# Attention and two feed-forward layers on one core: low part of x by PE and ACT for the first 8 units, word loads in turn, and layer 1's blocks 0 and 1 in two passes of steps

## The chip, the cores and the metric

The kernel runs on one core of a Trainium2 chip. The metric is the device time of one launch in microseconds (us). The engines are TensorE (PE, with its weight loads as PEld), VectorE (DVE), ScalarE (ACT), GpSimd (POOL) and SyncE (SP). SP and ACT issue the transfers (DMA) of this kernel; their queues are shown as SPq and ACTq. Each engine works through its own instructions in order.

## The reference

A linear attention with a decaying state, then two feed-forward layers, all in fp32:

```python
# q, k, v, alpha: (batch 4, heads 8, seq 768, head_dim 48)
state = alpha[:, :, t, :, None] * state + einsum('bhd,bhe->bhde', k[:, :, t], v[:, :, t])
y[:, :, t] = einsum('bhd,bhde->bhe', q[:, :, t], state)

x = y.transpose(0, 2, 1, 3).reshape(3072, 384)
h = x @ moe_w_in          # (384, 2048)
x = maximum(0.01 * h, h) @ moe_w_out
h = x @ moe2_w_in
out = where(h > 0, h, exp(minimum(h, 0)) - 1) @ moe2_w_out
```

## The kernel before, in words

**Units.** The attention is done in 24 units of 128 positions of one batch row (6 units a row, all 8 heads at once). A unit's inputs are a `pack` (alpha, k and q) and a `vt` (v); three buffers of each go round. Per unit, DVE scans alpha backward (`E`) and forward (`F`) and scales k and q with the scans; PE forms the scores (`sc`, two banks), turns k round (`pk`), and DVE masks the scores into `A`. PE multiplies A with v, and q with the carried state `T`, into `po`; k and v into `pu`, the state's increment. ACT copies `pk` (to `kn`) and casts `po` to the high part of x (`attn_xh`); DVE subtracts that from `po` to the low part (`attn_xl`). PE's fp32 products are made of such high and low parts (three products: high by high, low by high, high by low). All small PSUM results of a unit share three banks in turn (`ps_a`), so `pu` of the next unit takes the bank that `po` gives up.

**Quarters.** The first 8 units are written out by hand in `quarter(u, i)`, four quarters a unit; each prepares the next unit while it finishes its own. Units 0 to 3 (block 0) run ahead of all else, together with the conversions of the first weights. When a block's four units are done, `gather` moves 6 slices of x from partition to partition by DMA, since the heads do not fill the partitions.

**Steps.** A block is 512 rows of x. Layer 1 takes each block through 16 steps `m` of 128 of the 2048 inner columns: `ffn1_h` (nine products into `hp`), `ffn1_t` (ACT, 0.01 h), `ffn1_max` (DVE), `ffn1_gh` (ACT, high part), `ffn1_gl` (DVE, low part), and `ffn1_y` (nine products that add to three banks `y` over all 16 steps). At the last step `y` is copied to `x2t[block]`. The list `seq` holds the order of steps; PE does `ffn1_y` of step s and `ffn1_h` of step s + 2. There are 6 blocks, then layer 2 with 16 steps each likewise.

**Words.** The weights come as raw fp64 words and are converted on the chip, one step's w_in and w_out at a time: `stage1(m)` loads the words of step m with five DMAs on SP's queue, `convert_p` makes two passes on ACT, `convert_a` three instructions on DVE and ACT's cast to the high part, `convert_b` one subtraction on DVE for the low part. Layer 1's words are loaded into the tiles `x2t[0]` to `x2t[3]`, four steps in flight; `x2t[4]` and `x2t[5]` are scratch. The first sixteen steps, all of block 0, convert the words of the step that comes four later, and the quarters of block 1 are strewn among them (13 quarters over 14 steps). From the second block on all weights are there, and the units of the next block are strewn among the steps of a block.

Up to the end of that hand-made part, `in_order()` ties each engine to the order in which the code is written; behind it a scheduler may move instructions.

Of the kernel before, what the change touches and what calls it, by code (L numbers as in the profile page):

```python
# [10 lines left out]
I32 = mybir.dt.int32  # L11
# [8 lines left out]
def attention_two_layers_kernel(  # L20
# [42 lines left out]
    causal = const.tile([128, C], F32, name="causal")  # L63
    d0 = const.tile([PR, EXT], F32, name="d0")
# [19 lines left out]
    def constants():  # L84
        make_identity(nc, ident)
        nc.gpsimd.memset(causal, 1.0)
        nc.gpsimd.affine_select(
            out=causal, in_=causal, compare_op=ALU.is_ge, fill=0.0,
            base=0, pattern=[[1, C]], channel_multiplier=-1,
        )  # L90
        nc.vector.memset(d0, 0.0)
        nc.vector.memset(d0[:, 0:EXT:C + 1], 1.0)
        nc.vector.memset(d1, 0.0)
        nc.vector.memset(bias[:, 0:1], -1.0)
        nc.vector.memset(bias[:, 1:2], -ALPHA_SPAN)
        nc.vector.memset(far_sum[:, 1:2], 1.0)
# [144 lines left out]

    def attn_state(u):
        c = u % NC
        d = st[u]
        if c < NC - 1:
            Sn = at_p.tile([PR, NP, D], F32, tag="S", name="S")
            if c > 0:
                nc.vector.tensor_add(Sn, d["pu"], d["T"])
            else:
                nc.vector.tensor_copy(Sn, d["pu"])  # L250
            st["S"] = Sn
# [74 lines left out]

    def ffn1_y(j, m):
        n = xt[j][2]
        gh, gl = steps.pop((1, j, m))
        if m == 0:  # L330
            ytiles[j] = [ps_y.tile([128, n], F32, tag=f"y{c}", name=f"y{c}") for c in range(KD)]
        wh, wl = wout[m]
        for c in range(KD):
            for i, (a, x) in enumerate(((wh, gh), (wl, gh), (wh, gl))):
                nc.tensor.matmul(  # L335
                    ytiles[j][c], lhsT=a[:, c * 128:(c + 1) * 128], rhs=x,
                    start=(m == 0 and i == 0), stop=(m == KF - 1 and i == 2),
                )
        if m == KF - 1:
            t0 = blocks[j][0] * C  # L340
            dst = x2t[t0 // 512][:, :, t0 % 512:t0 % 512 + n]
            for c in range(KD):
                if c == 1:
                    nc.vector.tensor_copy(dst[:, c], ytiles[j][c])
                else:
                    nc.scalar.copy(dst[:, c], ytiles[j][c])
# [113 lines left out]
    def stage1(m, eng=None):  # L460
        t = x2t[m % 4].rearrange("p c f -> p (c f)").bitcast(I32)
# [42 lines left out]
    class Conversions:  # L504
# [20 lines left out]
        def b(self, upto):  # L525
            for i in range(self.done[2], min(upto, self.done[1])):
# [3 lines left out]
                if self.layer == 1 and m + 4 < KF:  # L530
                    stage1(m + 4)
# [121 lines left out]
    with ExitStack():  # L653
# [8 lines left out]
        for m in range(1, 4):  # L662
            stage1(m)
# [7 lines left out]
        def quarter(u, i, chain=True):  # L671
# [13 lines left out]
            elif i == 2:  # L685
# [6 lines left out]
                next_load(u + 3)  # L692
            else:
                attn_xl(u, xh, xl, off)
# [8 lines left out]
        for u in range(UB):  # L703
            for i in range(3):
                quarter(u, i)
            if u > 1:
                conv1.a(u - 1)
# [9 lines left out]
        quarter(UB, 1)  # L717
        conv1.b(UB - 1)
        ffn1_max(0, 0)
        ffn1_gh(0, 0)  # L720
        quarter(UB, 2)
        ffn1_h(0, 1)
        ffn1_t(0, 1)
        ffn1_gl(0, 0)
        conv1.p(UB)
        ffn1_max(0, 1)
        ffn1_gh(0, 1)
# [3 lines left out]
        seq = [(1, j, m) for j in range(NB) for m in range(KF)]  # L731
# [10 lines left out]
        for s, e in enumerate(seq):  # L742
# [3 lines left out]
            if s < KF:  # L746
# [9 lines left out]
                conv1.b(s + 4)  # L756
                ffn1_gl(n[1], n[2])
                conv1.p(s + 5)
                in_order()
                continue  # L760
            if ph == 1 and pieces:
                tgt = blocks[j + 1][1] * 4
                done = tgt - len([p for p in pieces if unit_block[p[0]] <= j + 1])
                want = min(tgt, -(-tgt * (m + 1) // (KF - LA)))
# [123 lines left out]
```

## Time and profile before

| | |
|---|---|
| time, median of 3 runs | 975.14 us (974.55 to 976.91) |
| the profiled execution | 976.15 us, span 974.4 us |
| PE busy | 922.9 us (95%) |
| PEld busy | 779.2 us (80%) |
| DVE busy | 532.4 us (55%) |
| ACT busy | 445.9 us (46%) |
| mean granted clock of PE | 0.974 |
| read from HBM, written | 54.37 MB, 4.72 MB |

The span runs from the first to the last instruction of the profiled execution; its own time is 1.75 us more. Busy shares are means over stages that have different limits. The granted clock is a share of 2.4 GHz; it has two levels, 1.2 and 2.4 GHz, so that 0.79 over a stretch is a mixture of both.

### The profile page before, as it was taken

How to read it: one execution, taken by the hardware profiler on the slowest of the kernel's cores; microseconds unless marked ns; L12 is line 12 of the kernel's file. 1: busy time of each engine (PE TensorE's matmuls, PEld its weight loads, DVE VectorE, ACT ScalarE, POOL GpSimd, SP SyncE). 2: the span in 40 equal slices, each digit the busy share in tenths (PEclk: the TensorE clock that was granted, in tenths of full speed). 3: DMA queues.
4: the chain of work that ended last, by engine and by line, in shares of the span. 5: the costliest groups of instructions: out<-in, count | busy, mean ns of one | idle time of the engine just before them, and what ended most of it. 6: DMA issues, size and time to landing. Idle time of an engine off the chain costs nothing.

```text
span 974.4 us, 13128 instructions
## 1 busy us (share of the span) xinstructions
PE 922.9 (95%) x5234; PEld 779.2 (80%) x5234; DVE 532.4 (55%) x876; ACT 445.9 (46%) x783; POOL 1.1 (0%) x8
## 2 busy tenths in 40 slices
PE   5678889999999999999999999999999999999996
PEld 4555666888788788788888889999999999899995
DVE  6769894855746556545369993433433433433332
ACT  1235653322322222233367795474564654644442
POOL 0000000000000000000000000000000000000000
PEclk9688998999999999999999999999999999999998
DMA  9664523113111212211134430020110200100001
GB/s 247 161 160 135 165 74 89 42 41 90 49 41 42 57 41 83 57 41 49 33 114 133 127 90 18 1 81 1 47 34 1 71 10 1 62 1 0 33 1 37
DMA packets 25093, 62.38 MB, mean 64 GB/s; under 512 B 3936, under 2 KB 7008, under 8 KB 25024
## 3 DMA queue, kind: packets, MB, share of 16 engines
q1 hardware_dynamic: 19184, 40.54, 14.8%
q10 hardware_dynamic: 5840, 20.92, 7.7%
q8 instruction: 43, 0.70, 0.3%
q14 instruction: 26, 0.21, 0.1%
HBM read 54.37 MB, written 4.72 MB: 61 GB/s over the span
## 4 chain that ended last, share of the span: by engine, by line
PE 84%; DVE 6%; DMA 6%; issue 1%; SPq 1%; ACT 1%; DVEq 0%; ACTq 0%
PE hp L364 21%; PE y L335 18%; PE hp L297 18%; PE oa L395 10%; PE o L395 10%; DMA x2t<-in_w_dram 2%; PE sc L158 2%; PE po L212 2%; PE po L218 2%; DMA vt<-in_vals_dram 2%; DVE x2t L276 1%; DVE x2t L278 1%; DMA pack<-in_seqs_dram 1%; DMA x<-x 1%; DVE x2t L275 1%
## 5 line engine op out<-in xcount | busy, mean ns | idle before, releaser
L297 PE MATMUL hp<-x,w 128*128 128x512 f32 x864 | 219.6, 397 | 14.8 <-DMA x<-x 7.4
L364 PE MATMUL hp<-x,w 128*128 128x512 f32 x864 | 215.4, 393 | 0.0
L297 PEld LDWEIGHTS hp<-x,w 128*128 128x128 f32 x864 | 162.2, 190 | 54.3 <-DVE w L282 8.0
L364 PEld LDWEIGHTS hp<-x,w 128*128 128x128 f32 x864 | 160.7, 188 | 29.3
L335 PE MATMUL y<-gh,w 128*128 128x512 f32 x576 | 179.8, 400 | 0.0
L373 DVE SCALAR_TENSOR_TENSOR t<-t,hp 128x512 f32<-128x512 f32 x96 | 65.9, 686 | 148.1 <-ACT t L372 148.1
L335 PEld LDWEIGHTS y<-gh,w 128*128 128x128 f32 x576 | 106.9, 191 | 23.5 <-issue 1.1
L303 ACT ACTIVATE t<-hp 128x512 f32<-128x512 f32 x96 | 57.2, 596 | 125.8 <-PE hp L297 125.6
L312 ACT CAST gh<-t 128x512 fp32r<-128x512 f32 x96 | 59.6, 621 | 113.3 <-PE y L335 61.7
L335 PE MATMUL y<-gl,w 128*128 128x512 f32 x288 | 109.9, 395 | 0.0
L308 DVE TENSOR_TENSOR t<-t,hp 128x512 f32<-128x512 f32 x96 | 65.4, 681 | 78.6 <-ACT t L303 78.6
L81 DVE TENSOR_TENSOR gl<-t,gh 128x512 fp32r<-128x512 f32 x96 | 66.4, 692 | 70.6 <-ACT gh L78 68.9
L371 ACT ACTIVATE t<-hp 128x512 f32<-128x512 f32 x96 | 57.1, 595 | 104.7 <-PE hp L364 104.7
L395 PE MATMUL oa<-w,gh 128*128 128x384 f32 x384 | 96.7, 337 | 0.0
L395 PE MATMUL o<-w,gh 128*128 128x384 f32 x384 | 94.6, 336 | 0.0
L318 DVE TENSOR_TENSOR gl<-t,gh 128x512 fp32r<-128x512 f32 x96 | 66.1, 689 | 47.6 <-ACT gh L312 44.6
L78 ACT CAST gh<-t 128x512 fp32r<-128x512 f32 x96 | 59.5, 620 | 64.7 <-PE oa L395 34.8
L395 PEld LDWEIGHTS o<-w,gh 128*128 128x128 f32 x384 | 70.6, 188 | 5.4
L395 PEld LDWEIGHTS oa<-w,gh 128*128 128x128 f32 x384 | 70.2, 188 | 2.9
L335 PEld LDWEIGHTS y<-gl,w 128*128 128x128 f32 x288 | 54.5, 189 | 12.1
L395 PE MATMUL oa<-w,gl 128*128 128x384 f32 x192 | 63.0, 337 | 0.0
L372 ACT ACTIVATE t<-t 128x512 f32<-128x512 f32 x96 | 60.8, 633 | 2.3
(91 smaller groups left out, 833.0 us busy)
## 6 DMA issues: line engine op xcount, KB each, us to landing
pack<-in_seqs_dram ACTq DMA_DIRECT2D x21, 674.2 KB, 5.6
stg<-in_w_dram SPq DMA_DIRECT2D x28, 384.0 KB, 3.2
x2t<-in_w_dram SPq DMA_DIRECT2D x20, 384.0 KB, 3.8
vt<-in_vals_dram ACTq DMA_DIRECT2D x21, 288.0 KB, 5.6
span<-in_seqs_dram SPq DMA_DIRECT2D x24, 226.2 KB, 2.6
x2t<-in_w_dram SPq DMA_DIRECT2D x32, 144.0 KB, 2.8
out_dram<-osb SPq DMA_DIRECT2D x24, 192.0 KB, 2.1
x<-x SPq DMA_DIRECT2D x36, 64.0 KB, 4.4
```

The costliest lines, as they stand in the source:

```text
L78: nc.scalar.copy(dst, src)
L81: (lo_engine or nc.vector).tensor_sub(lo, src, dst.bitcast(F32))
L297: nc.tensor.matmul(hp, lhsT=a[:, kk, :], rhs=x[:, kk, :n], start=(i == 0), stop=(i == 3 * KD - 1))
L303: nc.scalar.activation(t, steps[1, j, m], ACTF.Copy, scale=0.01)
L308: nc.vector.tensor_max(t, t, hp)
L312: nc.scalar.copy(gh, steps[1, j, m][0])
L318: nc.vector.tensor_sub(gl, t, gh.bitcast(F32))
L335: nc.tensor.matmul(ytiles[j][c], lhsT=a[:, c * 128:(c + 1) * 128], rhs=x, start=(m == 0 and i == 0), stop=(m == KF - 1 and i == 2),)
L364: nc.tensor.matmul(hp, lhsT=a[:, kk, :], rhs=x[:, kk, :], start=(i == 0), stop=(i == 3 * KD - 1))
L372: nc.scalar.activation(t, t, ACTF.Exp, scale=-1.0)
L373: nc.vector.scalar_tensor_tensor(out=t, in0=t, scalar=-1.0, in1=hp, op0=ALU.add, op1=ALU.max)
L395: nc.tensor.matmul(otiles[j][i], lhsT=a[:, i * 128:(i + 1) * 128], rhs=x, start=(m == 0 and n == 0), stop=(m == KF - 1 and n == 2),)
```

## The change

For units 0 to 7 the low part of x is no longer a DVE subtraction: PE adds the product of `minus` (the identity times -1) and the high part to `po` (`attn_rest`), and ACT copies what is left (`attn_xl_act`). The loads of the following units go to SP's queue. Only the words of step 0 are asked for ahead of the units; those of steps 1 to 3 follow one unit at a time, and from step 4 on two tiles, `x2t[2]` and `x2t[3]`, take turns. `hp` of step 1 stands ahead of the rest of unit 4.

The steps of layer 1 run as block 0 steps 0 to 3, block 1 steps 0 to 3, block 0 steps 4 to 15, block 1 steps 4 to 15. Blocks 0 and 1 therefore leave `y` twice: behind step 3 it is copied to `x2t[block]` by ACT, behind step 15 DVE adds it to that. All 13 quarters of block 1 stand in the first two entries of `seq`, and the 12 words left are converted in the entries 2 to 16, three in four. Block 2's units begin one entry later.

```diff
+        nc.scalar.activation(minus, ident[0:PR, 0:PR], ACTF.Copy, scale=-1.0)
...
+    def attn_rest(u, xh, off):
+        nc.tensor.matmul(st[u]["po"], lhsT=minus, rhs=xh[0:PR, :, off:off + C], start=False, stop=True,
+                         skip_group_check=True)
+
+    def attn_xl_act(u, xl, off):
+        nc.scalar.copy(xl[0:PR, :, off:off + C], st[u]["po"])
...
+    FIRST = 4
+
+    def parts(j, m):
+        return m == 0 or (j < 2 and m == FIRST), m == KF - 1 or (j < 2 and m == FIRST - 1)
...
-                if c == 1:
+                if j < 2 and m == KF - 1:
+                    nc.vector.tensor_add(dst[:, c], ytiles[j][c], dst[:, c])
+                elif c == 1 and j > 1:
                     nc.vector.tensor_copy(dst[:, c], ytiles[j][c])
                 else:
                     nc.scalar.copy(dst[:, c], ytiles[j][c])
...
-        t = x2t[m % 4].rearrange("p c f -> p (c f)").bitcast(I32)
+        t = x2t[m if m < 4 else 2 + m % 2].rearrange("p c f -> p (c f)").bitcast(I32)
...
-                if self.layer == 1 and m + 4 < KF:
-                    stage1(m + 4)
+                if self.layer == 1 and m >= 2 and m + 2 < KF:
+                    stage1(m + 2)
...
                 attn_xh(u, xh, off)
-                next_load(u + 3)
+                attn_rest(u, xh, off)
+                load_unit(u + 3)
+                load_v(u + 3)
             else:
-                attn_xl(u, xh, xl, off)
+                attn_xl_act(u, xl, off)
...
-        seq = [(1, j, m) for j in range(NB) for m in range(KF)]
+        head, tail = range(FIRST), range(FIRST, KF)
+        seq = [(1, j, m) for ms in (head, tail) for j in range(2) for m in ms]
+        seq += [(1, j, m) for j in range(2, NB) for m in range(KF)]
...
-            if s < KF:
+            if s <= KF:
+                c = 4 if s == 0 else 1 + FIRST + s - 2 - (s - 2) // 4 if s > 1 and s % 4 != 1 else 0
                 ffn1_y(j, m)
                 pe_h(n)
                 ffn1_t(n[1], n[2])
-                conv1.a(s + 4)
-                if s < KF - LA:
-                    for p in quarters[13 * s // (KF - LA):13 * (s + 1) // (KF - LA)]:
+                conv1.a(c)
+                if s < 2:
+                    for p in quarters[7 * s:7 * s + 7]:
```

Three places in the order of instructions show what moves. The first is DVE in the steps of layer 1, just behind the last quarters of unit 4. Names: `x2t` are words and scratch of a conversion, `w` the weights' parts, `t`, `gh` and `gl` those of a step, `x` the low part of a unit. Before, two conversions with a unit's scan behind the second:

```order
L275 TENSOR_SCALAR x2t_138<-x2t_134 128x768
L276 SCALAR_TENSOR_TENSOR x2t_138<-x2t_138 128x768
L278 ISA x2t_138<-x2t_134,x2t_138 128x1536
L240 TENSOR_TENSOR x<-po,x 112x4x128
L308 TENSOR_TENSOR t<-t,hp 128x512
L282 TENSOR_TENSOR w_4_111<-x2t_138,w_4_110 128x768
L318 TENSOR_TENSOR gl<-t,gh 128x512
L275 TENSOR_SCALAR x2t_139<-x2t_135 128x768
L276 SCALAR_TENSOR_TENSOR x2t_139<-x2t_139 128x768
L278 ISA x2t_139<-x2t_135,x2t_139 128x1536
L127 SCALAR_TENSOR_TENSOR E<-pack,d_96 112x517
```

With the change, the conversion of step 6 and what follows it:

```order
L284 TENSOR_SCALAR x2t_139<-x2t_137 128x768
L285 SCALAR_TENSOR_TENSOR x2t_139<-x2t_139 128x768
L287 ISA x2t_139<-x2t_137,x2t_139 128x1536
L317 TENSOR_TENSOR t<-t,hp 128x512
L291 TENSOR_TENSOR w_6_116<-x2t_139,w_6_115 128x768
L327 TENSOR_TENSOR gl<-t,gh 128x512
L317 TENSOR_TENSOR t<-t,hp 128x512
L327 TENSOR_TENSOR gl<-t,gh 128x512
L284 TENSOR_SCALAR x2t_140<-x2t_138 128x768
```

The subtraction for x and the scans of a unit are gone from between the conversions, and a step without a conversion (`t`, `gl` alone) has come in.

The second place is DVE in unit 2, the first unit with a conversion (`pack` is q being scaled, `E` the scan of unit 4). Before:

```order
L144 TENSOR_TENSOR pack<-pack,F 112x512
L275 TENSOR_SCALAR x2t_138<-x2t_134 128x768
L276 SCALAR_TENSOR_TENSOR x2t_138<-x2t_138 128x768
L278 ISA x2t_138<-x2t_134,x2t_138 128x1536
L240 TENSOR_TENSOR x<-po,x 112x4x128
L282 TENSOR_TENSOR w_0_103<-x2t_138,w_0_102 128x768
L127 SCALAR_TENSOR_TENSOR E<-pack,d_96 112x517
```

Now:

```order
L146 TENSOR_TENSOR pack<-pack,F 112x512
L284 TENSOR_SCALAR x2t_139<-x2t_135 128x768
L285 SCALAR_TENSOR_TENSOR x2t_139<-x2t_139 128x768
L287 ISA x2t_139<-x2t_135,x2t_139 128x1536
L291 TENSOR_TENSOR w_0_104<-x2t_139,w_0_103 128x768
L129 SCALAR_TENSOR_TENSOR E<-pack,d_97 112x517
```

Only the subtraction for x is gone; the conversion's last instruction now stands right behind its third.

The third place is SP's queue around the gather of block 1 (`x<-x`). Before, the words of the last step stand ahead of it and words of layer 2 behind:

```order
L467 DMA x2t_136<-in_w_dram 128x768
L465 DMA x2t_137<-in_w_dram 48x768
L466 DMA x2t_137<-in_w_dram 16x768
L465 DMA x2t_137<-in_w_dram 48x768
L466 DMA x2t_137<-in_w_dram 16x768
L467 DMA x2t_137<-in_w_dram 128x768
L262 DMA x<-x 16x2x512 x6
L481 DMA x2t_139<-in_w_dram 128x768 x2
```

Now the loads of units 9 and 10 stand ahead of it, and words of step 6 behind:

```order
L113 DMA pack<-in_seqs_dram 112x1541
L118 DMA vt<-in_vals_dram 128x576
L113 DMA pack<-in_seqs_dram 112x1541
L118 DMA vt<-in_vals_dram 128x576
L271 DMA x<-x 16x2x512 x6
L482 DMA x2t_137<-in_w_dram 48x768
L483 DMA x2t_137<-in_w_dram 16x768
```

The gather has moved ahead of ten steps' words, and directly behind two units' loads.

## Rows read from the trace of the kernel before

**Rows 1.** Busy time by stretch: length, busy us and count per engine, granted clock, DMA, GB/s

```profile
0.00:66.49 66.49, 38.89 (x358) 30.82 (x359) 46.54 (x79) 15.48 (x22) 1.14 (x8) 0.79 0.81 207
66.49:167.71 101.22, 85.86 (x433) 65.10 (x432) 81.65 (x117) 53.17 (x77) 0.00 (x0) 0.92 0.39 112
167.71:966.00 798.29, 798.11 (x4446) 683.26 (x4444) 403.68 (x681) 377.04 (x684) 0.00 (x0) 1.00 0.16 46
```

**Rows 2.** Waits of PE, 0 to 210 us: us in total, times, longest

```profile
PE pk L166 <- DVE A L180: 10.6, 3, 4.6
...
PE hp L297 <- DVE w L282: 5.8, 4, 2.1
```

**Rows 3.** Timeline, steps of block 0: start, duration, instruction, idle before and releaser

```profile
102.30 0.55 DVE L275 TENSOR_SCALAR x2t<-x2t 128x768 int32<-128x768 int32 x1
...
102.49 2.20 PE L297 MATMUL hp<-x,w 128*128 128x512 f32 x9
...
106.57 2.20 PE L297 MATMUL hp<-x,w 128*128 128x512 f32 x9
...
107.60 0.55 DVE L275 TENSOR_SCALAR x2t<-x2t 128x768 int32<-128x768 int32 x1
```

**Rows 4.** Timeline, units 0 to 3

```profile
16.29 1.16 PE L158 MATMUL sc<-pack 48*128 48x128 f32 x16
16.41 0.58 ACT L237 CAST x<-po 112x512 fp32r<-112x512 f32 x1 [1.31 <-PE po L212]
...
17.64 1.23 DVE L127 TENSOR_TENSOR_SCAN E<-pack,d 112x517 f32<-112x517 f32 x1
...
20.05 1.28 DVE L180 TENSOR_TENSOR A<-sc,causal 128x512 f32<-128x512 f32 x2
...
30.08 1.23 DVE L127 TENSOR_TENSOR_SCAN E<-pack,d 112x517 f32<-112x517 f32 x1 [3.15 <-DMA pack<-in_seqs_dram]
...
32.49 1.28 DVE L180 TENSOR_TENSOR A<-sc,causal 128x512 f32<-128x512 f32 x2
...
42.58 1.28 DVE L180 TENSOR_TENSOR A<-sc,causal 128x512 f32<-128x512 f32 x2
```

**Rows 5.** Timeline, gathers of blocks 0 and 1 and the hp behind each

```profile
47.63 0.32 ACTq L111 DMA_DIRECT2D pack<-in_seqs_dram  x1
...
49.11 3.93 SPq L262 DMA_DIRECT2D x<-x  x6
...
54.95 4.77 PE L297 MATMUL hp<-x,w 128*128 128x512 f32 x9 [5.15 <-DMA x<-x]
...
156.59 3.78 SPq L262 DMA_DIRECT2D x<-x  x6
...
159.68 0.47 PE L297 MATMUL hp<-x,w 128*128 128x512 f32 x1 [0.68 <-DMA x<-x]
```

**Rows 6.** Timeline of DVE, unit 3: low part and end of a conversion

```profile
48.40 0.68 DVE L240 TENSOR_TENSOR x<-po,x 112x512 fp32r<-112x512 f32 x1
49.38 0.96 DVE L282 TENSOR_TENSOR w<-x2t,w 128x768 fp32r<-128x768 f32 x1 [0.30 <-ACT w L279]
```

**Rows 7.** The stretch of unit 1, and T's product there and in unit 4

```profile
17.64:30.08 12.44, 8.47 (x84) 6.96 (x84) 6.30 (x13) 2.80 (x4) 0.00 (x0) 0.58 1.02 256
...
23.62 1.95 PE L218 MATMUL po<-pack,T 48*48 48x128 f32 x16
...
61.11 1.08 PE L218 MATMUL po<-pack,T 48*48 48x128 f32 x16
```

**Rows 8.** Issues of one word; landing of words, 66 to 150 and 12 to 30 us

```profile
72.61 0.31 SPq L465 DMA_DIRECT2D x2t<-in_w_dram  x1
...
74.36 0.42 SPq L467 DMA_DIRECT2D x2t<-in_w_dram  x1
...
x2t<-in_w_dram SPq DMA_DIRECT2D x9, 384.0 KB, 3.6
...
x2t<-in_w_dram SPq DMA_DIRECT2D x3, 384.0 KB, 6.1
```

More of the change, by code (lines that the diff above doesn't have):

```diff
@@ L63, in attention_two_layers_kernel @@
     causal = const.tile([128, C], F32, name="causal")
+    minus = const.tile([PR, PR], F32R, name="minus")
     d0 = const.tile([PR, EXT], F32, name="d0")
@@ L329, in ffn1_y @@
         gh, gl = steps.pop((1, j, m))
-        if m == 0:
+        first, last = parts(j, m)
+        if first:
             ytiles[j] = [ps_y.tile([128, n], F32, tag=f"y{c}", name=f"y{c}") for c in range(KD)]
@@ L336, in ffn1_y @@
                     ytiles[j][c], lhsT=a[:, c * 128:(c + 1) * 128], rhs=x,
-                    start=(m == 0 and i == 0), stop=(m == KF - 1 and i == 2),
+                    start=(first and i == 0), stop=(last and i == 2),
                 )
-        if m == KF - 1:
+        if last:
             t0 = blocks[j][0] * C
@@ L661, in attention_two_layers_kernel @@
         load_v(2)
-        for m in range(1, 4):
-            stage1(m)
         order1 = [("both", m) for m in range(KF)]
@@ L705, in attention_two_layers_kernel @@
                 quarter(u, i)
+            if u < 3:
+                stage1(u + 1)
             if u > 1:
@@ L717, in attention_two_layers_kernel @@
         quarter(UB, 1)
+        ffn1_h(0, 1)
+        ffn1_t(0, 1)
         conv1.b(UB - 1)
+        quarter(UB, 2)
         ffn1_max(0, 0)
         ffn1_gh(0, 0)
-        quarter(UB, 2)
-        ffn1_h(0, 1)
-        ffn1_t(0, 1)
+        ffn1_max(0, 1)
+        ffn1_gh(0, 1)
         ffn1_gl(0, 0)
         conv1.p(UB)
-        ffn1_max(0, 1)
-        ffn1_gh(0, 1)
         ffn1_gl(0, 1)
         in_order()
-        seq = [(1, j, m) for j in range(NB) for m in range(KF)]
+        head, tail = range(FIRST), range(FIRST, KF)
+        seq = [(1, j, m) for ms in (head, tail) for j in range(2) for m in ms]
+        seq += [(1, j, m) for j in range(2, NB) for m in range(KF)]
         seq += [(2, j, m) for j in range(NT // 512) for m in range(KF)]
@@ L755, in attention_two_layers_kernel @@
                 ffn1_gh(n[1], n[2])
-                conv1.b(s + 4)
+                conv1.b(c)
                 ffn1_gl(n[1], n[2])
-                conv1.p(s + 5)
+                if c:
+                    conv1.p(c + 1)
                 in_order()
@@ L761, in attention_two_layers_kernel @@
             if ph == 1 and pieces:
-                tgt = blocks[j + 1][1] * 4
-                done = tgt - len([p for p in pieces if unit_block[p[0]] <= j + 1])
-                want = min(tgt, -(-tgt * (m + 1) // (KF - LA)))
+                nb = max(j + 1, 2)
+                tgt = blocks[nb][1] * 4
+                done = tgt - len([p for p in pieces if unit_block[p[0]] <= nb])
+                i, of = (s - KF, KF - LA - 1) if s < 2 * KF else (m + 1, KF - LA)
+                want = min(tgt, -(-tgt * i // of))
                 now, pieces = pieces[:max(0, want - done)], pieces[max(0, want - done):]
```

## The prediction

> **What bounds the kernel now.** I read the busy times by stretch first. From 167.71 to 966 us TensorE (PE) is busy in 798.1 of 798.3 us at the full granted clock [rows 1]: nothing that leaves that work unchanged can gain or lose there. What can move lies ahead of it. Up to 66.49 us, where the first product with w_out starts, PE is busy 38.89 us at a granted clock of 0.79; from there to 167.71 us, the end of block 0's sixteen steps, 85.86 of 101.22 us at 0.92, while VectorE (DVE) is busy 81.65 us [rows 1].
>
> The waits of PE say on whom it waits: most on DVE's mask A (10.6 us ahead of pk alone) and on DVE's low part of the weights (5.8 us) [rows 2]. So DVE sets the pace of the first 167 us. A step of layer 1, y and hp, costs PE 4.08 us, from one hp to the next (102.49 to 106.57) where nothing else lies between; DVE goes from one conversion to the next in 5.30 us (102.30 to 107.60), with no attention in between but one low part of x [rows 3]. Sixteen such steps plus the attention of block 1 make the 101 us.
>
> **The early units.** I take the order of the change and put the durations of the trace on it.
> Unit 0: the low part on DVE needs po and ACT's copy of it (at 16.41), and only behind it E of unit 2 runs, at 17.64; A of unit 1 follows at 20.05 [rows 4]. With the low part gone from DVE, E to T are done while PE is still at po, and A(1) can start when sc(1) is there, which runs from 16.29 for 1.16 us [rows 4]: A(1) at 17.5, 2.55 us gained.
> Unit 1: E of unit 3 waits 3.15 us for its pack, until 30.08 [rows 4]. ACT issued its load behind the words of four steps; now it stands on SP's queue ahead of all words but the first, and its buffer has been free since unit 0's products. That wait goes. But PE now has to do the product with minus (of 512 columns, 0.47 us for one such alone [rows 5]), and ACT the copy (0.58 us, as the x cast [rows 4]), before pu may take po's bank; before, one subtraction on DVE (0.68 us [rows 6]) did it. I charge 1.0 us per unit where PE's chain sets the pace, as it now does in unit 1. Chain: A(1) 17.5, pu 19.3, pk 20.3, po and the product with T 3.9 us, sc 2.0 us, A(2) at 26.3 instead of 32.49: 6.2 us gained.
> Units 2 and 3: nothing. From A(2) to A(3) are 10.09 us, all DVE with one conversion [rows 4]. There the low part runs from 48.40, behind the third instruction of a conversion, and the conversion's last starts at 49.38 after 0.30 us more of waiting for ACT's cast [rows 6]. The low part is inside a wait that stays; taking it away frees no time.
> The first products come in another order, gl(0,0) now behind the maximum of step 1; by durations that costs 0.5 us. So y(0,0) starts at 66.49 - 6.2 + 0.5 = 60.8 us.
>
> **Steps 0 and 1** now hold 13 quarters of block 1's attention, which were spread over 14 steps. Little else is there to do meanwhile, so it is a chain. From y(0,0): DVE has gl 0.6, conversion 2.65, E to T 2.4, A(5) 0.7 to its first half: 6.9 us with gaps. Then pk, po, T's product and sc: 4.4 us at the full clock, 7.0 us at half (T's product: 1.08 against 1.95 us [rows 7]). Then product with minus, copy and pu 1.75 to 2.15; pk and po 2.15 to 3.0; y(0,1) and hp(0,3) 4.1 to 8; sc 1.16 to 2.1; and behind hp(0,3) ACT's t, x, PE's product, ACT's copy, pu, po, T's product, x and the last product with minus 5.7 to 7. Sum: 26.2 us at the full clock, 36 at half. In the units before, up to 66.49 us, the granted clock is 0.79 [rows 1], that is 42% of the time at 1.2 GHz and the rest at 2.4; 26.2 + 0.42 x 9.8 = 30.3. The steps' products make this one denser, so I take 29.3: y(0,2) at 90.1 us.
>
> **The gather.** hp of (block 1, step 0) is now the product right behind y(0,2). It needs block 1's x, whose last low part ends 0.7 us after y(0,2) begins. Block 0's gather, issued at 49.11 with a pack in flight since 47.63, let hp start at 54.95, 5.84 us later, and that hp took 4.77 us; block 1's, issued at 156.59 with no such load near, let the first go at 159.68, 3.09 us later [rows 5]. In the new order the loads of units 9 and 10 stand right ahead of the gather on SP's queue, and the last of them can only be issued when unit 7 has used its pack, some 2 us before. So I take 5.84: hp(1,0) ends at 90.1 + 0.7 + 5.84 + 4.77 = 101.4 us; without a wait it would be 94.2. The Trainium skill, "DMA: Bandwidth & Descriptors", section "Queues, rings and completion order", says that a copy's semaphore increment lands only after every earlier write of that DMA engine, on any of its queues. By that rule the gather waits out the loads ahead of it; the two gathers of the trace agree (5.84 against 3.09 us). With 3.09 the sum would be 2.75 us better.
>
> **Steps 2 to 16** convert 12 words in 15 steps, three steps in four, with no attention. DVE needs 5.1 to 5.3 us from conversion to conversion [rows 3] (the low part of x lay in the wait for ACT's cast there too), and 1.9 us in the step without one (two instructions of 0.6 us and the wait for gh): 3 x 5.2 + 1.9 = 17.5 us against PE's 16.3, so 4.38 a step. From the end of hp(1,0) to the end of y in step 15 there are 12.5 steps: 54.8 us; if DVE is hidden, 51. ACT has six copies of y more (0.58 us each, as its copy of po [rows 4]), in steps 3 and 7 ahead of its other work; PE waits for y's banks there, 1.7 us as I lay it out. Sum 56.5: step 15 ends at 157.9 us.
> Words: two buffers now instead of four. A word's fifth and last piece is issued 1.75 us behind its first and lands 3.6 us later [rows 8]; with 1.8 us of ACT's two passes and 1.1 us of DVE until the buffer is free again, that is 8.3 us a buffer, 4.15 a word, and 5.2 are to be had. At nothing, therefore; the cover is 1 us a word. The three DVE additions per block in place of copies, 0.7 us each, fall in steps without conversion: nothing.
>
> **Sum.** 167.7 - 157.9 = 9.8 us, less 0.3 for the one conversion left in step 16: 9.5. The attention of block 2 starts a step later, under a full PE, at nothing (if it were late, PE would wait on A, as in [rows 2]). The profiled execution took 976.15 us (span 974.4); with the change 966.65, which against the median of 975.14 is 965.6 us.
>
> **Rivals.**
> All goes well (957 to 961 us): the gather lands in 3.1 us and DVE hides under PE at 4.08 a step: 2.75 + 3.8 us better, 959.1. For it: PE runs ahead by two steps, so a slow step is evened out; against it: the DVE sum is above PE's. Chance 0.2.
> The clock stays low (972.3 us): all of steps 0 and 1 at 1.2 GHz, 36 instead of 29.3 us. For it: 0.58 in the stretch of unit 1, where PE also works in bursts [rows 7]; against it the 0.79 of all units. The Trainium skill, "TensorE: Matmul & The Clock Gate", Part 1, calls the low clock the default that only activity releases; the trace agrees in the 0.58 and, since 0.79 is not 0.5, not in all of it. Chance 0.1.
> The words come late, slower than before: if a landing takes 6.3 us rather than 3.6, a buffer turns in 11 us, a word in 5.5 us, and 12 words take 66 us instead of 56.5, which eats all 9.5; that is the point from which it decides. At 7.2 us, twice the 3.6, a word takes 5.95 us, 12 words 71.4, and the time is 965.6 + 14.9 = 980.5 us. For it: 6.1 us for the same pieces in that crowded stretch; against it: 3.6 between 66 and 150 us, where words are asked for as fast [rows 8]. Chance 0.07.
> The order gains nothing, since the attention was hidden below the steps and is now bare: steps 0 and 1 cost 29.3 us where they cost 9.5, and the rest must win that back at 4.38 a step. It is dead if the steps with conversions still take 5.3 us and more each: 12.5 x 5.3 = 66 us, 975 us, no change. Chance 0.08.
> My forecast with its own range, 962 to 970, holds 0.55.
>
> **Numbers.** 965.6 us; 957 to 971.5 leaves out about 2 in 10. A difference within 0.3% (2.9 us) can hardly be told from none. Faster 0.85, same 0.08, slower 0.07.
>
> **What would show it.** A(2) near 26 us and E(3) without a wait for pack; y(0,0) near 61; y(0,2) near 90 with A and sc alternating in PE's waits; one wait of PE for x of 5 to 8 us near 92 to 100; conversions 5.1 to 5.3 us apart with a longer pause in each fourth step; no wait of ACT for words behind 100 us; step 15's y done near 158, and from there the same row of products as before. Wrong if ACT waits for words, if DVE's steps are longer than 5.3, or if the attention chain of steps 0 and 1 is far from 29 us.

## The result, and the profile after

| | before | after |
|---|---|---|
| median | 974.86 us (974.55 to 976.91, 4 runs) | 961.69 us (960.84 to 961.84, 4 runs) |
| profiled execution, span | 976.15, 974.4 us | 960.84, 959.1 us |
| last product ends at | 965.83 us | 952.30 us |

The ratio of the times is 0.9859, 95% interval 0.9842 to 0.9876: 13.2 us faster by the medians. The two profiled executions differ by 15.3 us; their last products by 13.5. The other 1.8 lie behind the last product (8.57 us before, 6.80 after), where only the output is copied out and lands, so I compare at the last product.

The busy time by stretch of the kernel after, cut where its steps cut it: the start of y of step 0 of block 0, which I write y(0,0), the start of y(0,2), the end of hp(1,0), and the end of y of the sixteenth entry of the list of steps. Columns: length, then busy us and count of PE, PEld, DVE, ACT, POOL, the granted clock, DMA, GB/s.

```profile
0.00:61.25 61.25, 42.14 (x363) 32.20 (x363) 44.02 (x76) 18.30 (x29) 1.14 (x8) 0.80 0.76 197
61.25:85.52 24.27, 20.33 (x192) 15.35 (x192) 22.66 (x37) 10.50 (x17) 0.00 (x0) 1.00 0.50 124
85.52:95.74 10.22, 6.79 (x20) 4.77 (x19) 3.08 (x4) 1.10 (x2) 0.00 (x0) 0.76 0.76 211
95.74:151.33 55.59, 53.73 (x225) 42.12 (x224) 45.71 (x61) 38.91 (x59) 0.00 (x0) 0.98 0.39 114
151.33:959.10 807.77, 798.94 (x4446) 683.14 (x4445) 414.55 (x696) 381.05 (x689) 0.00 (x0) 1.00 0.16 48
```

Beside [rows 1], y(0,0) comes 5.24 us earlier (61.25 against 66.49), and the sixteen entries that follow take 90.08 us instead of 101.22: 16.38 us. From there to the last product it takes 800.97 us where it took 798.12, so 2.85 are given back, and 13.53 remain. In the second stretch DVE is busy 22.66 of 24.27 us: the attention of three units has become a chain that leaves DVE almost no gap, at a full clock.

The timeline of DVE in units 1 to 3, which answers to [rows 4, 6] (start, duration, instruction, idle before and releaser):

```profile
18.84 1.29 DVE L182 TENSOR_TENSOR A<-sc,causal 128x512 f32<-128x512 f32 x2 [1.05 <-PE sc L160]
...
23.45 1.23 DVE L129 TENSOR_TENSOR_SCAN E<-pack,d 112x517 f32<-112x517 f32 x1 [1.33 <-DMA pack<-in_seqs_dram]
...
25.86 1.28 DVE L182 TENSOR_TENSOR A<-sc,causal 128x512 f32<-128x512 f32 x2
...
32.66 0.96 DVE L291 TENSOR_TENSOR w<-x2t,w 128x768 fp32r<-128x768 f32 x1 [0.90 <-ACT w L288]
...
35.95 1.28 DVE L182 TENSOR_TENSOR A<-sc,causal 128x512 f32<-128x512 f32 x2
```

A of unit 1 now waits for its scores, so PE's chain paces there; A of unit 2 starts at 25.86. From A(2) to A(3) it is 10.09 us, to the hundredth what it was: the low part did lie in a wait, and that wait is now the 0.90 us ahead of L291.

The gather of block 1 and hp(1,0) behind it, with the loads ahead of them ([rows 5] had block 0's gather behind a pack, and a gather with nothing near):

```profile
84.55 0.31 SPq L113 DMA_DIRECT2D pack<-in_seqs_dram  x1
84.91 0.43 SPq L118 DMA_DIRECT2D vt<-in_vals_dram  x1
86.33 3.79 SPq L271 DMA_DIRECT2D x<-x  x6
...
91.17 4.57 PE L306 MATMUL hp<-x,w 128*128 128x512 f32 x9 [3.43 <-DMA x<-x]
```

DVE in the steps with conversions, the last of three and the step without one ([rows 3] had 5.30 us from conversion to conversion):

```profile
103.70 0.55 DVE L284 TENSOR_SCALAR x2t<-x2t 128x768 int32<-128x768 int32 x1
...
109.92 0.69 DVE L317 TENSOR_TENSOR t<-t,hp 128x512 f32<-128x512 f32 x1 [1.05 <-ACT t L312]
111.30 0.69 DVE L327 TENSOR_TENSOR gl<-t,gh 128x512 fp32r<-128x512 f32 x1 [0.69 <-ACT gh L321]
111.91 0.56 DVE L284 TENSOR_SCALAR x2t<-x2t 128x768 int32<-128x768 int32 x1
...
116.83 0.56 DVE L284 TENSOR_SCALAR x2t<-x2t 128x768 int32<-128x768 int32 x1
...
121.93 0.56 DVE L284 TENSOR_SCALAR x2t<-x2t 128x768 int32<-128x768 int32 x1
```

Conversions stand 5.10 us apart (116.83 to 121.93), and 8.21 across the step without one (103.70 to 111.91), in which DVE waits 1.05 and 0.69 us for ACT. Four entries thus take DVE 18.23 us (103.70 to 121.93), 4.56 each. PE doesn't wait for that from the start: it stands idle for only 1.86 of the 55.59 us of this stage, and the y of its second entry and of the fifth, three entries on, stand 12.24 us apart, 4.08 an entry, which is PE's own pace in [rows 3]:

```profile
100.64 0.61 PE L350 MATMUL y<-gh,w 128*128 128x512 f32 x2
...
112.88 0.61 PE L350 MATMUL y<-gh,w 128*128 128x512 f32 x2
```

The waits of PE from 0 to 200 us, beside [rows 2], and the two places behind the sixteenth entry where time is given back:

```profile
PE sc L160 <- DVE pack L146: 8.7, 1, 8.7
PE hp L306 <- DMA x<-x: 6.6, 4, 3.4
...
PE pk L168 <- DVE A L182: 2.4, 1, 2.4
```

```profile
151.79 2.64 PE L306 MATMUL hp<-x,w 128*128 128x512 f32 x9 [0.46 <-ACT w L288]
...
156.89 2.65 PE L306 MATMUL hp<-x,w 128*128 128x512 f32 x9 [0.41 <-ACT w L288]
...
181.10 0.70 PE L350 MATMUL y<-gh,w 128*128 128x512 f32 x2 [1.11 <-DVE x2t L359]
```

The wait for A ahead of pk fell from 10.6 to 2.4 us; what PE waits for most, after the first scores, is now the gather.

### The profile page after: what moved, and what is told of

Same layout as the page of the kernel before. It is cut to its first block, busy times and chain, and to the rows that moved or that the text cites. A ratio compares the mean times of both kernels' runs of the same rounds, so it can differ in the third digit from the quotient of the medians.

```text
span 959.1 us, 13157 instructions
## 1 busy us (share of the span) xinstructions
PE 921.9 (96%) x5242; PEld 777.6 (81%) x5242; DVE 530.0 (55%) x872; ACT 449.9 (47%) x794; POOL 1.1 (0%) x8
## 4 chain that ended last, share of the span: by engine, by line
PE 83%; DVE 6%; DMA 4%; ACT 4%; issue 1%; SPq 1%; DVEq 0%; ACTq 0%
PE hp L381 21%; PE y L350 17%; PE hp L306 17%; PE oa L412 11%; PE o L412 11%; DMA pack<-in_seqs_dram 3%; PE po L214 2%; PE sc L160 2%; PE po L220 2%; DVE x2t L285 1%; DVE x2t L287 1%; DVE E L129 1%; PE pu L233 1%; ACT w L288 1%; ACT x2t L279 1%
## 5 line engine op out<-in xcount | busy, mean ns | idle before, releaser
L381 PEld LDWEIGHTS hp<-x,w 128*128 128x128 f32 x864 | 160.7, 188 | 29.3
L82 DVE TENSOR_TENSOR gl<-t,gh 128x512 fp32r<-128x512 f32 x96 | 66.5, 692 | 70.0 <-ACT gh L79 68.4
```

The lines of the kernel that those rows point to most:

```text
L82: (lo_engine or nc.vector).tensor_sub(lo, src, dst.bitcast(F32))
L381: nc.tensor.matmul(hp, lhsT=a[:, kk, :], rhs=x[:, kk, :], start=(i == 0), stop=(i == 3 * KD - 1))
```

## The experiments

All kernels are the changed kernel with one edit, unless a line says more, and all compute the whole result. Each ratio is to the kernel before on the same chip, with its 95% interval. The stages are those of the first table of the profile after, from each kernel's profiled execution; entry 15 is the sixteenth of the list. In the two rows marked one pass the sixteen entries are all of block 0, and one figure stands for them together.

| kernel | median us | ratio (interval) | y(0,0) at | steps 0 and 1, clock | to end of hp(1,0) | to end of entry 15 |
|---|---|---|---|---|---|---|
| changed | 961.69 | 0.9859 (0.9842, 0.9876) | 61.25 | 24.27, 1.00 | 10.22 | 55.59 |
| f1, changed again | 961.84 | 0.9869 (0.9846, 0.9893) | 57.62 | 25.07, 0.93 | 9.99 | 55.56 |
| e1, low part on DVE | 974.26 | 0.9978 (0.9964, 0.9992) | 62.47 | 32.24, 0.82 | 11.31 | 55.56 |
| e2, loads as before | 971.10 | 0.9944 (0.9922, 0.9966) | 67.52 | 27.86, 0.82 | 10.30 | 55.58 |
| e3, one pass | 972.71 | 0.9962 (0.9946, 0.9978) | 57.71 | 108.47 together | | |
| h4, one pass and low part on DVE | 969.96 | 0.9938 (0.9920, 0.9956) | 62.94 | 100.35 together | | |
| e4, gather first | 958.42 | 0.9820 (0.9797, 0.9843) | 56.47 | 27.86, 0.82 | 10.13 | 55.59 |
| f3, gather by two queues | 959.57 | 0.9860 (0.9832, 0.9889) | 56.51 | 25.10, 0.93 | 11.64 | 55.57 |
| f2, ACT's passes late | 958.66 | 0.9832 (0.9813, 0.9851) | 58.83 | 27.85, 0.82 | 11.00 | 54.06 |
| f4, low part of w on GpSimd | 968.65 | 0.9941 (0.9918, 0.9963) | 57.10 | 25.10, 0.93 | 11.15 | 60.85 |
| h1, e4 and f3 | 955.25 | 0.9784 (0.9766, 0.9803) | 56.94 | 24.26, 1.00 | 10.02 | 55.84 |
| h2, h1 and f2 | 952.39 | 0.9758 (0.9738, 0.9778) | 56.49 | 25.12, 0.93 | 9.31 | 53.97 |
| h3, h2 and y(0,3) first | 951.14 | 0.9744 (0.9725, 0.9762) | 56.27 | 24.27, 1.00 | 10.39 | 51.75 |

In h3 hp(1,0) and hp(1,1) run as one group, so the last two columns are cut one hp later; together they are 62.14 us, against 63.28 in h2.

**The same kernel again (f1).** No edit.

> The changed kernel itself, unedited, beside the others of this group on the same chip and with more runs, since its first runs were made elsewhere. Expected 961.7 us, the ratio to before 0.986; where its steps 0 and 1 meet the low clock, as in the run with the gather first, they take 27 to 28 us instead of 24.3.

The time repeats, the early part doesn't: y(0,0) lies at 57.62 in this execution and at 61.25 in the other. Here E of unit 3 starts at 21.30 us with no wait, there at 23.45 with 1.33 us for its pack. So differences of up to 3.6 us in y(0,0) between single profiles say nothing about an edit. From the end of hp(1,0) to the end of entry 15 the executions agree to 0.03 us.

**The low part back on DVE (e1).**

```diff
                 attn_xh(u, xh, off)
-                attn_rest(u, xh, off)
...
-                attn_xl_act(u, xl, off)
+                attn_xl(u, xh, xl, off)
```

> The changed kernel with the low part of x of units 0 to 7 back on VectorE (no product with minus, no copy by ACT); all else as changed. My theory: the move pays only where DVE is not converting (units 0 and 1, 2.5 us, less about 1 us for the longer chain of PE and ACT) and a little in steps 0 and 1: 963 to 964 us, A of unit 2 near 27.5 us instead of 25.9. Rival, that the low part is the main gain of the early units: 966 us or more. Rival, that the product and the copy cost what they save: 961.7, as changed.

A miss by 10 us: nearly the whole gain is gone. In the early units it costs about what the prediction had it for, 6.2 us less the 3.15 of the pack: A(2) comes at 28.80 us, 2.9 us behind the first execution of the changed kernel and 5.1 behind f1; y(0,0) comes at 62.47, 1.2 and 4.9 us behind. But the larger loss stands in steps 0 and 1, 32.24 us against 24.27 and 25.07, where I had looked for little. DVE there, e1 (x<-po is the low part, L129 the next unit's scan E, which is queued behind it):

```profile
74.39 0.69 DVE L242 TENSOR_TENSOR x<-po,x 112x512 fp32r<-112x512 f32 x1 [1.94 <-ACT x L239]
...
86.61 0.69 DVE L242 TENSOR_TENSOR x<-po,x 112x512 fp32r<-112x512 f32 x1 [4.14 <-ACT x L239]
87.22 1.23 DVE L129 TENSOR_TENSOR_SCAN E<-pack,d 112x517 f32<-112x517 f32 x1
...
95.45 0.69 DVE L242 TENSOR_TENSOR x<-po,x 112x512 fp32r<-112x512 f32 x1 [2.55 <-ACT x L239]
```

DVE stands still for ACT's copy of po, and the scans of the next unit stand behind it. In the changed kernel DVE goes from one unit to the next with no wait longer than 0.4 us (0.74 in f1). The clock of e1 is low there too, 0.82. Three kernels with 0.82 in these steps and the low part off DVE (e2, e4, f2) take 27.86 us; an estimate from these is that of the 8 us 4.4 are the order on DVE (32.24 - 27.86) and 3.6 the clock (27.86 - 24.27). That the order pulls the clock down isn't shown, since those three have it without that order.

**The loads as before (e2).** Words of four steps ahead of the units, the units' loads on ACT's queue.

```diff
+        for m in range(1, 4):
+            stage1(m)
...
-                load_unit(u + 3)
-                load_v(u + 3)
+                load_unit(u + 3, eng=nc.scalar)
+                load_v(u + 3, eng=nc.scalar)
...
-            if u < 3:
-                stage1(u + 1)
```

> The changed kernel with the loads of units on ACT's queue again and the words of steps 0 to 3 all asked for at the start; all else as changed. My theory: E of unit 3 waits again some 4 us for its pack, A of unit 2 comes near 29.5 us, and everything behind it is later by 3 to 4 us: 965 us. Rival, that the words' order is without weight: 961.7 us.

Slower by more than expected. DVE in unit 1 of e2:

```profile
18.31 1.29 DVE L182 TENSOR_TENSOR A<-sc,causal 128x512 f32<-128x512 f32 x2 [1.05 <-PE sc L160]
...
29.03 1.23 DVE L129 TENSOR_TENSOR_SCAN E<-pack,d 112x517 f32<-112x517 f32 x1 [7.44 <-DMA pack<-in_seqs_dram]
...
31.44 1.28 DVE L182 TENSOR_TENSOR A<-sc,causal 128x512 f32<-128x512 f32 x2
```

A(1) is early, but E(3) waits 7.44 us where the kernel before waited 3.15 [rows 4]: the pack lets it start only 1.05 us sooner (29.03 against 30.08), so most of what the low part gave ahead of it is waited away, and A(2) is at 31.44 (32.49 before). The two edits of the early part need each other. A(2) tells it more surely than y(0,0): with both edits it comes at 22.7 to 25.9 us in the ten executions that have them, with the loads alone at 28.8 (e1) and 29.4 (h4), with the low part alone at 31.4, with neither at 32.5. In y(0,0): both 56.3 to 61.3 (some of them with another gather), loads alone 62.5 and 62.9, low part alone 67.5, neither 66.5.

**One pass of steps (e3), and the loads alone (h4).** Both take the list of steps and the conversions back; h4 puts the low part back on DVE as well, as in e1. Both keep hp of step 1 ahead of the rest of unit 4, as the changed kernel has it.

```diff
-        head, tail = range(FIRST), range(FIRST, KF)
-        seq = [(1, j, m) for ms in (head, tail) for j in range(2) for m in ms]
-        seq += [(1, j, m) for j in range(2, NB) for m in range(KF)]
+        seq = [(1, j, m) for j in range(NB) for m in range(KF)]
...
-                if s < 2:
-                    for p in quarters[7 * s:7 * s + 7]:
+                if s < KF - LA:
+                    for p in quarters[13 * s // (KF - LA):13 * (s + 1) // (KF - LA)]:
```

> The early part of the change alone (low part by PE and ACT, loads and words in turn, hp of step 1 ahead), but layer 1 in one pass a block, four word buffers, and block 1's quarters strewn over 14 steps as before. My theory: y of step 0 starts at 61.3 us as in the changed kernel, and the sixteen steps take about their 101 us as before, so 974.9 - 5.2 = 969.7 us; the other 8 us of the gain come from the two passes. Rival, that the steps too get shorter since the low part has left DVE there (0.6 us a unit, 4 units): 967.5 us.

> Edit: of the change only the loads on SP's queue and the words asked for in turn; low part on DVE and one pass of sixteen steps per block as in the kernel before. Theory, E of unit 3 loses its wait for the pack (3.15 us before) and y(0,0) starts near 62.5, the sixteen steps take 101 us as before or more, since the quarters come at the same rate: 971 to 973, that is 3 us faster than before at most. Rival, the low part off DVE is worth several us in the early units too: then this is no faster than before (974 to 976), with e3_one_pass at 972.7 beside it.

e3 starts y(0,0) at 57.71, 8.8 us before the kernel before, and loses most of it again: its sixteen steps take 108.47 us against 101.22 [rows 1]. h4, with less of the change, is the faster of the two, 6.4 us below the kernel before where I had given it 3 at most, and its steps take 100.35. So with one pass of steps the low part on PE and ACT is no gain: 5.2 us earlier at y(0,0) (57.71 against 62.94), 8.1 us longer in the steps. Whether it is a loss is not quite clear, since the intervals of the two ratios overlap. DVE's waits in the sixteen steps, e3 and then h4 (us in total, times, longest):

```profile
DVE t L317 <- ACT t L312: 23.2, 8, 8.0
```

```profile
DVE t L317 <- ACT t L312: 13.7, 6, 5.8
```

The maximum t waits for ACT's t, and that for PE's hp, 38.6 us in e3 and 30.9 in h4; PE in e3 waits 3.5 us for ACT's copy of x ahead of the added product, a wait that h4 doesn't have. That hp is late through this added link of PE and ACT I infer from those waits; no run took the link alone out of the steps.

**The gather.** Three edits: the loads of units 6 and 10 behind it (e4), its six copies by two queues in turn (f3), both (h1, whose diff is shown).

```diff
-    def gather(x, n):
+    def gather(x, n, two=False):
...
-            nc.sync.dma_start(x[hi:hi + 16, :, b // 2, :n].bitcast(F32), x[lo:lo + 16, :, KD, :n].bitcast(F32))
+            (nc.scalar if two and b % 2 else nc.sync).dma_start(x[hi:hi + 16, :, b // 2, :n].bitcast(F32), x[lo:lo + 16, :, KD, :n].bitcast(F32))
...
-                load_unit(u + 3)
-                load_v(u + 3)
+                if u % 4 != 3:
+                    load_unit(u + 3)
+                    load_v(u + 3)
...
-                    gather(t, blocks[j][1] * C)
+                    gather(t, blocks[j][1] * C, True)
+                    load_unit(u + 3)
+                    load_v(u + 3)
```

> The changed kernel with the loads of the unit that follows a block's last (units 6 and 10) issued behind the gather instead of ahead of it. My theory: the gather waits out the loads ahead of it; without them block 1's x is there 3.1 us after the issue instead of 4.8, PE waits 1.7 us instead of 3.4, and block 0's gather gains 1 us too: 959.5 us. Rival, that the gather's time is its own: 961.7 us. Rival, that the late loads of unit 10 hold something up: above 961.7.

> The changed kernel with three of the six copies of the first two gathers issued by ACT instead of SP. My theory: hp waits for the last copy, and that is late because SP issues the six one behind another in 3.8 us; with two queues hp ends 7.5 us after the first issue instead of 9.4, at both gathers: 958 us. Rival, that the landing behind the loads of units sets it: 961 to 962 us.

> Edit: the loads of units 6 and 10 go behind the gather, and the gather's six copies are issued in turn by SP and ACT. Theory, two limits lie on the gather's path one over the other, the loads in flight ahead of it (they set the landing, 2.7 to 4.3 us against 2.3 to 2.5 without them, 6.1 to 6.3 with the loads issued close ahead) and the serial issues of six copies on one queue (3.8 to 4.2 us): with both gone the last copy is issued about 2 us behind the first and lands in 2.3 us, so that hp(1,0) ends 7 to 7.5 us after the end of y(0,2) plus 0.8, that is 8 us in place of 10.1; time 956.5 to 958.5. Rival, copies of both queues share what carries them, so that six copies land no sooner however they are issued: hp(1,0) ends as with the loads moved alone, 10.1 us behind y(0,2)'s start, time 958.4 to 960.

How the copies of block 1's gather land (KB each, median us from issue to landing), the changed kernel, e4, f3 and h1:

```profile
x<-x SPq DMA_DIRECT2D x6, 64.0 KB, 3.6
```

```profile
x<-x SPq DMA_DIRECT2D x6, 64.0 KB, 2.3
```

```profile
x<-x SPq DMA_DIRECT2D x3, 64.0 KB, 6.1
x<-x ACTq DMA_DIRECT2D x3, 64.0 KB, 6.3
```

```profile
x<-x SPq DMA_DIRECT2D x3, 64.0 KB, 2.6
x<-x ACTq DMA_DIRECT2D x3, 64.0 KB, 3.0
```

With the loads 1.8 us ahead, two queues land no sooner than one: hp's products start 6.57 us after the first issue in f3, 4.84 in the changed kernel, and f3's hp ends 10.8 us after it, not 7.5. There the theory of the serial issue fails, and f3's time can't be told from f1's. The load of vt ahead lands at 88.4 us in f3 and at 89.9 in the changed kernel, and the first copy right behind it, at 88.7 and 90.7. The Trainium skill, "DMA: Bandwidth & Descriptors", section "Queues, rings and completion order", has a copy's increment land only after every earlier write of that DMA engine on any queue; the copies that ACT issued in f3 agree, which landed 6.3 us after their issue, behind loads on SP's queue.

With the loads behind, a copy lands in 2.3 to 3.0 us in the median. But e4 gains nothing at hp(1,0), where PE still waits 3.32 us in all, 1.7 having been expected:

```profile
88.20 0.47 PE L306 MATMUL hp<-x,w 128*128 128x512 f32 x1 [1.61 <-DMA x<-x]
...
89.83 0.77 PE L306 MATMUL hp<-x,w 128*128 128x512 f32 x1 [1.16 <-DMA x<-x]
...
91.14 3.32 PE L306 MATMUL hp<-x,w 128*128 128x512 f32 x7 [0.55 <-DMA x<-x]
```

Seven of the nine products stand behind the last copy: `ffn1_h` takes the three slices of x in turn, the last two copies fill the third slice, so the third product needs them, and the six others follow it in order. The kernel before shows the same at block 1's gather, behind the x1 of [rows 5] and with no load near:

```profile
162.21 2.66 PE L297 MATMUL hp<-x,w 128*128 128x512 f32 x7 [0.76 <-DMA x<-x]
```

In the changed kernel, f1, e4 and h1 alike the third product starts 0.13 us after the last copy has landed, and hp ends 3.2 to 3.5 us after that landing. The loads ahead delay the first copy (4.3 us to land, 2.3 in e4) but hardly the last (2.7 and 2.3): it lands 5.95 us after the first issue in the changed kernel and 5.87 in e4. Kernels with the gather unedited take 9.99 to 11.15 us in this stage (changed, f1, f2, f4), so that differences of about 1 us there say nothing. e4's time is nevertheless 3.3 us below the changed kernel's, where 2.2 were expected; the interval of its ratio touches that of the changed kernel and lies just apart from f1's. Its profile doesn't show where the gain lies, since it ends entry 15 at 150.05 us, between f1 (148.24) and the changed kernel's first execution (151.33).

In h1 too hp(1,0) waits in three pieces:

```profile
82.01 1.89 SPq L271 DMA_DIRECT2D x<-x  x3
82.01 2.16 ACTq L271 DMA_DIRECT2D x<-x  x3
...
84.00 0.51 SPq L113 DMA_DIRECT2D pack<-in_seqs_dram  x1
...
84.85 0.49 PE L306 MATMUL hp<-x,w 128*128 128x512 f32 x1 [1.40 <-DMA x<-x]
...
85.84 0.47 PE L306 MATMUL hp<-x,w 128*128 128x512 f32 x1 [0.50 <-DMA x<-x]
...
87.90 3.32 PE L306 MATMUL hp<-x,w 128*128 128x512 f32 x7 [1.58 <-DMA x<-x]
```

1.40 + 0.50 + 1.58 are 3.48 us, as in the changed kernel (3.43), and hp(1,0) ends 9.2 us after the first issue, not 7 to 7.5. My theory of two limits fell here, and the rival's 10.1 us from the start of y(0,2) come out (10.02), though not for its reason: five copies land sooner than in e4, and the last takes 4.2 us to land, with the pack of unit 10 issued 0.44 us behind it. In h2, with the same gather, it takes 3.5, and the stage 9.31. That the pack delays it is likely, not shown. The time of h1, 955.25, is nevertheless lower than that of the changed kernel: the intervals of the two ratios lie apart. One place may show in the profile: block 0's gather, which the same edit touches, brings y(0,0) 22.10 us behind A(3) (34.84 to 56.94), against 25.30 in the changed kernel and 23.83 in f1; but h2, with the same edit, has 23.69. Most of the 6 us isn't located; it may be in the executions that were not profiled, since h1's profiled one (956.71) is its slowest and f1's (958.46) its fastest.

**ACT's passes late (f2, h2).** In three steps of four ACT makes two passes over the next word behind gh. In every fourth step they are moved behind gl of the step without a conversion, so that ACT's t there isn't queued behind them.

```diff
-                if c:
+                if c and (s % 4 or s == 0):
                     conv1.p(c + 1)
+                elif s % 4 == 1 and s > 1:
+                    conv1.p(conv1.done[1] + 1)
```

> The changed kernel with ACT's two passes over the next words moved from ahead of t to behind gl in the steps without a conversion (entries 5, 9 and 13). My theory: steps 2 to 16 are paced by VectorE, and in each step without a conversion it waits 1.0 us for t because ACT makes the passes first; that wait goes, 3 us in all: 958.7 us, and from the end of hp(1,0) to the end of y in entry 15 some 52.6 us instead of 55.6. Rival, that TensorE or the words set the pace there: 961.7, 55.6 us.

> Edit: as h1, and ACT's two passes over the words stand behind gl in the steps without a conversion. Theory, two savings in different stretches add up: 1.5 us from the end of hp(1,0) to the end of y of entry 15 (54.1 in place of 55.6) and about 0.9 in the two entries behind; time 2 to 2.5 us below h1, 954.5 to 956. Rival, what the one saves is waited for in the other place: within 1 us of h1.

The 1.05 us that DVE waited for ACT's t in the step without a conversion are 0.19 in f2:

```profile
111.00 0.69 DVE L317 TENSOR_TENSOR t<-t,hp 128x512 f32<-128x512 f32 x1 [0.19 <-ACT t L312]
```

The long stage loses 1.5 us and the two entries behind it 0.94 (8.66 us from the end of entry 15 to y of entry 17, instead of 9.60): 2.4 us of the 3 that I had expected. From the conversion at 103.70 to that at 148.33, 44.63 us in the changed kernel, DVE itself takes 41.98 in f2 (105.64 to 147.62), 2.65 less; so most of what DVE gains reaches PE by entry 17. The medians of f2 and f1 differ by 3.2 us, but the intervals of their ratios overlap. On top of h1 the same edit gives 1.87 us in the long stage and 0.95 in the two entries behind (8.64 instead of 9.59 us), 2.8 in all; the medians differ by 2.86, again with overlapping intervals. Both places of the theory show, and the size is a little above the 2 to 2.5 us expected.

**y(0,3) into the wait (h3).**

```diff
-                ffn1_y(j, m)
+                if s != 3:
+                    ffn1_y(j, m)
+                if s == 2:
+                    ffn1_y(*seq[3][1:])
```

> Edit: as h2, and y(0,3) is put ahead of hp(1,0), into the wait for the gather. Theory, DVE paces the steps that follow, so that what TensorE does early is waited for later: 0 to 1 us below h2. Rival, TensorE paces what follows: the 2.1 us of that product fill the wait and come off the time.

PE now does y(0,3) from 84.23 on, after 1.43 us of waiting for its gh, and then finds all of x there:

```profile
84.23 0.74 PE L350 MATMUL y<-gh,w 128*128 128x512 f32 x2 [1.43 <-ACT gh L321]
...
86.68 4.25 PE L306 MATMUL hp<-x,w 128*128 128x512 f32 x18
```

From y(0,2) to the end of entry 15 it is 1.14 us less than in h2, and 1.25 by the medians, though the intervals of h2 and h3 overlap. That lies between what a pace of DVE (0 to 1) and a pace of PE (2.1) would give. h3 is the fastest kernel of the study, 951.14 us, 1.2% below the changed one by the ratios.

**The weights' low part on GpSimd (f4).** A test of what paces the steps with conversions: the 11 DVE instructions of 0.96 us for the words of steps 5 to 15 go elsewhere.

```diff
-                convert_b(*self.open.pop(i))
+                convert_b(*self.open.pop(i), eng=nc.gpsimd if self.layer == 1 and i > 4 else None)
```

> The changed kernel with the low part of the weights of steps 5 to 15 subtracted by GpSimd instead of VectorE. By my theory VectorE paces steps 2 to 16, so without 0.9 us in each conversion they come to TensorE's 4.08 us a step: 52 us instead of 55.6 and 958.5 us. Rival: GpSimd takes more than 3 us for it, the low part is late for hp of the last steps, and the time is 962 to 966 us.

Slower, by 5.3 us in that stage. GpSimd and DVE in f4:

```profile
105.86 1.85 POOL L291 TENSOR_TENSOR w<-x2t,w 128x768 fp32r<-128x768 f32 x1 [4.12 <-ACT w L288]
...
106.33 1.92 DVE L327 TENSOR_TENSOR gl<-t,gh 128x512 fp32r<-128x512 f32 x1 [0.82 <-ACT gh L321]
...
109.77 0.69 DVE L327 TENSOR_TENSOR gl<-t,gh 128x512 fp32r<-128x512 f32 x1 [0.69 <-ACT gh L321]
```

The instruction takes 1.85 us on GpSimd, and DVE's gl, started beside it, ends 0.54 us after GpSimd is done (108.25 against 107.71), at 1.92 instead of 0.69 us. It stands as if held until the other has finished. PE's waits for gl ahead of y are 5.9 us in this stage, and 0.9 in the changed kernel. The Trainium skill, "SBUF — State Buffer", section "Who interferes with whom", says that a DVE instruction with two SBUF inputs contends with a GpSimd instruction that reads SBUF, and that the one behind blocks; the trace agrees. So the edit put a new wait on the path, and does not tell whether DVE is the pace.

## Why the prediction was right, and where it was not

The direction held, and 961.69 us lies within 957 to 971.5; it is 3.9 us below the 965.6 named and just below the likeliest case's own range of 962 to 970. That it comes so near is partly luck, since two errors go against each other: steps 0 and 1 were 5.0 us shorter than summed, and 2.55 us were given back at places that the sum had at nothing. By its steps:

- **The early units.** A(2) was to come at 26.3 and came at 25.86; y(0,0) at 60.8, came at 61.25 and in f1 at 57.62. That A(2) fits so well is luck: A(1) came at 18.84 instead of 17.5, and PE's chain from there to the end of sc(2) took 6.4 us (18.84 to 25.23) where I had 8.8, mostly since I put po, T's product and sc at the half clock. What held A(2) was DVE's wait for the pack; f1, without it, has 23.71. The loads were said to end the wait for the pack; they left 1.33 us of it in one execution and none in the other. That the low part in units 2 and 3 sat in a wait is right (10.09 us from A(2) to A(3) in both kernels).
- **Steps 0 and 1**, 29.3 us, measured 24.27: the term that was mis-sized most. Two parts: my chain was 26.2 at the full clock, where rows at 1.00 show 24.27, and I took the clock of the units before, 0.79, where the profile shows 1.00. Kernels with the same instructions there show 0.93 (25.1 us) and 0.82 (27.9), so part of the 5 us is the execution's and not the kernel's.
- **The gather.** I took 5.84 us from first issue to hp's start and 4.77 for hp, and it was 4.84 and 4.57; with the 0.81 us up to the issue the stage is 10.22 where I had 11.31. The mechanism was only half right. That loads ahead delay the copies' landing is shown (e4, f3). That without them the sum would be 2.75 us better is refuted: e4 has 10.13 us. I had compared the start of all nine products (5.84) with that of the first of nine (3.09, an x1 in [rows 5]). Seven products of that hp begin 5.62 us after the first issue (156.59 to 162.21), with no load near. What holds hp is the landing of the last copy, and so in e4 the issue of six copies one behind another; what delays it once they go by two queues (h1) stays open. An order of the nine products that leaves the third slice's three for the end was not tried.
- **The steps with conversions**, 56.5 us for 12.5 steps, measured 55.59. Conversions 5.10 us apart, as from the rows. But the step without a conversion takes 3.11 us (8.21 - 5.10) where I had 1.9: the 1.05 us for ACT's t, queued behind its passes, was left out. Three such steps are 3.6 us that the sum lacks. They don't show in it because PE goes at its own 4.08 us in the first entries, and because the wait for y's banks is 0.88 us (L363, at 118.00) where I had 1.7; so this near hit is luck too. That DVE is the pace in the later entries is borne out by f2 (2.4 us) and in part by h3; f4 was spoilt by its own wait. The words are hidden with two buffers, as the sum had them: ACT's only waits for words up to 200 us, 2.7 us in all, come behind the last word of layer 1.
- **Behind entry 15** I charged 0.3 us; it is 2.85. PE waits 0.46 + 0.41 us for ACT's high part of the last words, and 1.11 us for DVE's additions of y, which I had costed at nothing; together 1.98. The next y needs the banks that the additions read, so it waits for them. The rest is PE's own busy time, 798.94 us where it was 798.11 [rows 1].
- The terms add up: 0.45 late at y(0,0), 5.03, 1.09 and 0.91 better in the next three stages make the end of entry 15 come at 151.33, 6.6 us ahead of 157.9; 2.55 more are given back behind it. The prediction's 9.5 and 4.0 more are the 13.5 at the last product.

The reason I gave for moving the low part, the early units, was half of it or less. By e1 it is worth 1.2 to 4.9 us at y(0,0) and 7.2 to 8.0 in steps 0 and 1 (32.24 against 25.07 and 24.27), some of it the clock. That it pays there because the two passes make the attention a chain without gaps is argued from e1's waits, and from e3 against h4, where in one pass it brings nothing. So the parts are no sum. The loads alone, with hp of step 1 ahead, bring 6.4 us (h4); any two of the three parts bring 1.7 to 4.9 (medians against before: e1 1.7, e3 3.3, e2 4.9); all three bring 13. The two passes alone and the low part alone were not run, nor the kernel with hp of step 1 at its old place.

Open remain what sets the clock in steps 0 and 1, where the gains of e4 and h1 lie, and what delays the last copy in h1.

## What to carry to other kernels

Before moving work off an engine, look at what is queued behind it there, not only at its duration: subtractions of 0.7 us on DVE cost some 4.4 us in steps 0 and 1, by the estimate above, where the next unit's scans stood behind their waits, and nothing in units 2 and 3, where they sat in another wait. Parts of a change can have the sign of their neighbours: measure them together and apart before dropping or keeping one. Where a wait is for several transfers, ask which one most of the work needs, the first or the last: here seven of nine products stood behind the last. And where a wait is the bound, fill it with a product that is ready (y(0,3)), rather than only shorten it.

## What was unexpected

- The same instructions of steps 0 and 1 ran at a granted clock of 1.00, 0.93 or 0.82 of 2.4 GHz in different executions, in 24.3, 25.1 or 27.9 us. The profiles don't show what decides it.
- Six copies of 64 KB took 3.79 us to issue on one queue, and 1.89 and 2.16 us, side by side, on two.
- DVE's gl took 1.92 us beside an instruction of GpSimd, and 0.69 without.
- The end of the output, behind the last product, took 8.57 us in one execution and 6.80 in the other; with the same instructions it is 6.7 to 7.1 us in twelve of the fourteen profiled executions and 8.6 in two (before and e2).
